# Output weights in two runs of 32 KB per partition, half the array's rows for each KV group, and three groups' projections in the bank of w2's sums

## The chip, the cores and the metric

The kernel runs on one core of a Trainium2 chip. The metric is the device time of one execution in microseconds (us), given as a median of several executions. The span of a profile is about 2 us shorter than the device time (before: 398.7 us of 400.74). The granted clock is the share of its full clock that PE was given, as the profile lists it.

Engines in the profile: PE is the matmul engine, PEld its weight loads, DVE, ACT and POOL the others, SPq the queue from which almost all transfers are issued. A transfer is spread over 16 transfer engines.

## The reference, cut to what matters

One token of a decode step: a layer norm, an attention with 32 query heads over 4 KV groups and 65,536 cached keys (k_cache and v_cache are 4 x 65536 x 128 in bf16, 67 MB each), an output projection, and beside it a small mixer with an MLP.

```python
def reference(A_x, A_k_cache, A_v_cache, A_wq, A_wo, B_x, B_w1, B_w2, B_w3, B_w4):
    # _A_ref: q = x @ wq; softmax(q k^T / sqrt(128)) v, 8 query heads per KV group;
    #         o.reshape(1, 1, 4096) @ wo                      wo: 4096 x 1024
    # _B_ref: h = gelu(ln(x) @ w1), shifted, @ w2; x1 = x + hs
    #         x1 + gelu(ln(x1) @ w3) @ w4                     w4: 3584 x 1024
    xn = _layernorm(x, axis=-1)
    return x + _A_ref(xn, ...) + _B_ref(xn, ...)
```

## The kernel before

Everything is read once through three slots of 64 KB per partition, in a fixed order: wq, w3, w1 and w2, then K and V tiles of 8.39 MB in turn, with wo between the last K and the last V, and w4 in four pieces at the end. A slot is loaded anew as soon as its user is done.

```python
W4_PIECES = (8, 14, 5, 1)
FIRST = 8
# ... cut ...
    stream = ["wq", "w3", "w12"]
    for u in range(NU):
        if u == NU - 1:
            stream += [("K", u), "wo", ("V", u)]
        else:
            stream += [("K", u), ("V", u)]
    stream.append("w4")
# ... cut: in Stream.load ...
            elif it == "wo":
                go(out=t[:].rearrange("p (g n) -> p g n", g=HKV),
                   in_=A_wo.rearrange("(g p j) n -> p g (j n)", g=HKV, p=P))
            elif it == "w4":
                w4_v = B_w4.rearrange("(m c) n -> m c n", c=FC)
                c0 = 0
                for n in W4_PIECES:
                    go(out=t[:, c0 * D:(c0 + n) * D], in_=w4_v[:, c0:c0 + n, :].rearrange("p c n -> p (c n)"))
                    c0 += n
```

The projections of groups 0 to 2 go, row by row, into a bank that the last scores also use; the last group's goes straight into the final sums (`quarter_acc`), as w4's products do.

```python
    def project(g):
        wt = st.tiles["wo"][:].rearrange("p (g j n) -> p g j n", g=HKV, j=8)
        for j in range(8):
            for h2 in range(2):
                if g == HKV - 1:
                    mm = quarter_acc(oT[g][:, j:j + 1], wt[:, g, j, 512 * h2:512 * (h2 + 1)], h2)
                    continue
                nc.tensor.matmul(tail["rows"][0:1, h2, :], lhsT=oT[g][:, j:j + 1],
                                 rhs=wt[:, g, j, 512 * h2:512 * (h2 + 1)], start=(g == 0 and j == 0),
                                 stop=(g == HKV - 2 and j == 7), tile_position=(0, 0))
        return mm.ins if g == HKV - 1 else None

    def quarter_acc(lhsT, row, j):
        for h in range(2):
            q = 2 * h + j
            mm = nc.tensor.matmul(quarters[h][32 * q:32 * q + 32, 0:256], lhsT=lhsT.to_broadcast([P, 32]),
                                  rhs=row[:, 256 * h:256 * (h + 1)], start=False, stop=False,
                                  tile_position=(0, 32 * q), skip_group_check=True)
        return mm
# ... cut ...
    compute_v(NU - 1, first_rows)                 # last V tile, then w4's first piece
    # ... then the last group's projection, then w4's pieces 2 to 4: compute_w4(8, 28), 80 matmuls
```

## Time and profile before

| | before |
|---|---|
| device time, first three runs | 400.97 us (400.63 to 401.44) |
| span of the profile | 398.7 us |
| last K tile landed | 340.57 us |
| wo landed | 323.68 + 36.3 = 360.0 us |
| last V tile's matmuls start | 379.43 us |
| w4's pieces 2 and 3 landed | 392.8 and 362.6 + 33.2 = 395.8 us |
| PE's last matmul ends | 396.84 us |

From the page of the kernel before: the first line, the engines' busy time, and the queue table (queue and kind, packets, MB, share of 16 engines' span).

```profile
span 398.7 us, 2684 instructions
...
PE 225.5 (57%) x1416; PEld 45.9 (12%) x922; DVE 210.7 (53%) x160; ACT 27.0 (7%) x35; POOL 5.8 (1%) x29
...
q1 hardware_dynamic: 3984, 169.87, 98.9%
q8 instruction: 9, 0.15, 0.1%
...
big<-in_A_wo_dram SPq DMA_DIRECT2D x1, 8192.0 KB, 36.3
...
big<-in_B_w_dram SPq DMA_DIRECT2D x1, 1280.0 KB, 33.2
```

The first queue is busy for 98.9% of the span: the kernel streams 170 MB and does all else beside it.

The chain of waits of before, its end (start, length, what):

```profile
362.16 30.64 DMA big<-in_B_w_dram
392.80 0.04 issue
392.84 4.05 PE pm_r L473 x80
396.89 0.02 issue
396.92 0.43 DVE out_t L520
```

PE waits for w4's second piece until 392.8 us and then goes through the 80 last matmuls in one sweep; pieces 3 and 4 land just in time. The matmuls on PE in that part (start, length, engine, line, operation, count, and in brackets the idle time before it and what ended it):

```profile
367.64 12.02 PE L455 MATMUL o_acc<-big,oT 128*1 128x512 bf16 x45 [2.40 <-ACT p_sb L380]
...
379.93 3.83 PE L412 MATMUL oacc<-big,p_sb 128*32 128x512 bf16 x58
...
387.96 1.06 PE L473 MATMUL pm_r<-big,oT 128*32 128x256 bf16 x32 [1.07 <-DVE oT L446]
392.84 4.00 PE L473 MATMUL pm_r<-big,hT 128*32 128x256 bf16 x80 [3.82 <-DMA big<-in_B_w_dram]
```

### The profile page before, as it was taken

To read this page: it belongs to the slowest core of one execution; us is meant where nothing else is said; L and a number is where in the kernel's file an instruction comes from. 1 tells how busy PE (TensorE), PEld (TensorE's weight loads), DVE (VectorE), ACT (ScalarE), POOL (GpSimd) and SP (SyncE) were. 2 spreads that over 40 slices of the span, in tenths; PEclk is the share of its full clock that TensorE was granted. 3 is DMA by queue.
4 is the path that set the end of the run, shared out by engine and by line. 5 is a ranking of instruction groups with operands and counts; after the bars stand their busy time and mean duration, and the time that the engine had idled before them with its cause. 6 is when DMAs were issued, how large, how long until landed. Compare 5 with 4: busy or idle time off the path is not lost.

```text
span 398.7 us, 2684 instructions
## 1 busy us (share of the span) xinstructions
PE 225.5 (57%) x1416; PEld 45.9 (12%) x922; DVE 210.7 (53%) x160; ACT 27.0 (7%) x35; POOL 5.8 (1%) x29
## 2 busy tenths in 40 slices
PE   0261960691668256923974196529552944394974
PEld 0210000010200120001001010200020101010133
DVE  0611010965196549653963895259439932894150
ACT  1001010003000200020002000200010011002000
POOL 2000000000000000000000000000000000000000
PEclk9995995597669666978796789568867997698896
DMA  9998999999999999999999999999999999999996
GB/s 421 421 443 382 439 441 473 447 421 421 416 435 421 441 447 455 421 421 427 436 421 427 454 454 427 416 427 427 434 436 454 434 434 388 419 452 426 418 432 252
DMA packets 4000, 170.03 MB, mean 426 GB/s; under 512 B 403, under 2 KB 405, under 8 KB 534
## 3 DMA queue, kind: packets, MB, share of 16 engines
q1 hardware_dynamic: 3984, 169.87, 98.9%
q8 instruction: 9, 0.15, 0.1%
q14 instruction: 1, 0.01, 0.0%
q10 hardware_dynamic: 6, 0.00, 0.0%
HBM read 169.87 MB, written 0.00 MB: 426 GB/s over the span
## 4 chain that ended last, share of the span: by engine, by line
DMA 55%; DVE 24%; PE 15%; ACT 2%; another core or an unknown queue 2%; issue 1%; SPq 0%; DVEq 0%; ACTq 0%
DMA big<-in_A_k_cache_dram 42%; DVE big L357 19%; PE sc L362 8%; DMA big<-in_B_w_dram 8%; DMA big<-in_A_wq_dram 5%; PE oacc L412 4%; DVE p_sb L383 2%; DVE mx L367 2%; ACT p_sb L380 2%; PE psq L287 2%; PE pm_r L473 1%; PE pm_mx L369 0%; DVE m L371 0%; PE pm_mx L376 0%
## 5 line engine op out<-in xcount | busy, mean ns | idle before, releaser
L362 PE MATMUL sc<-big,qdiag 128*128 128x512 bf16 x512 | 129.2, 413 | 65.5 <-DVE big L357 60.0
L357 DVE STREAM_TRANSPOSE big<-big 128x4096 f32<-128x4096 f32 x32 | 139.4, 4412 | 50.3 <-DMA big<-in_A_k_cache_dram 50.3
L412 PE MATMUL oacc<-big,p_sb 128*32 128x512 bf16 x512 | 44.9, 521 | 34.5 <-DVE p_sb L383 34.5
L367 DVE TENSOR_REDUCE mx<-sc 128x1 f32<-128x2048 f32 x8 | 18.3, 2292 | 29.8 <-PE sc L362 29.8
L362 PEld LDWEIGHTS <-qdiag 128*128 128x128 bf16 x128 | 13.2, 103 | 177.1 <-issue 145.6
L380 ACT ACTIVATE p_sb<-sc,nball 128x2048 bf16<-128x2048 f32 x8 | 15.7, 1967 | 220.0 <-DVE nball L378 219.9
L383 DVE STREAM_TRANSPOSE p_sb<-p_sb 128x2048 bf16<-128x2048 bf16 x8 | 18.5, 2311 | 18.0 <-ACT p_sb L380 18.0
L412 PEld LDWEIGHTS <-p_sb 128*32 128x32 bf16 x512 | 16.8, 126 | 59.5 <-DVE p_sb L383 35.1
L287 PE MATMUL psh<-big,ln_rep_b 128*32 128x512 bf16 (+1 forms) x64 | 12.4, 942 | 7.6 <-DMA big<-in_B_w_dram 7.6
L455 PE MATMUL o_acc<-big,oT 128*1 128x512 bf16 x48 | 12.7, 433 | 2.4 <-ACT p_sb L380 2.4
L369 PE MATMUL pm_mx<-ident_f,mx 128*1 128x128 f32 x8 | 2.3, 282 | 19.1 <-DVE mx L367 19.1
L421 DVE SCALAR_TENSOR_TENSOR og<-oacc,wb,og 128x512 f32<-128x512 f32 x4 | 3.0, 751 | 18.1 <-PE oacc L412 18.1
L326 DVE STREAM_TRANSPOSE h_row<-h_row 128x896 bf16<-128x896 bf16 x1 | 1.1, 1111 | 20.8 <-ACT h_row L325 20.8
L287 PE MATMUL psq<-big,ln_rep_a 128*32 128x512 bf16 x64 | 6.2, 575 | 3.8 <-DMA big<-in_A_wq_dram 3.8
L238 PE MATMUL pm_ln<-ln_rowsum_a,ones_f 128*128 128x1 f32 x2 | 0.6, 348 | 12.7 <-DVE ln_rowsum_a L236 12.7
L311 POOL COPY qdiag<-qx 32x32 bf16<-32x32 bf16 x16 | 3.2, 203 | 279.0 <-PE sc L362 249.8
L473 PE MATMUL pm_r<-big,hT 128*32 128x256 bf16 x112 | 5.1, 345 | 3.8 <-DMA big<-in_B_w_dram 3.8
L229 DVE STREAM_TRANSPOSE x_t<-x_row 32x256 bf16<-32x256 bf16 x4 | 2.5, 616 | 8.3 <-DMA x_row<-in_A_x_dram 8.2
L466 DVE TENSOR_TENSOR big<-o_acc,big 1x512 f32<-1x512 f32 x2 | 1.4, 680 | 9.8 <-PE o_acc L455 9.7
L434 PE MATMUL pm_e<-ol,sel8big 128*128 128x129 f32 x6 | 1.7, 372 | 7.9 <-DVE ol L432 7.9
L299 DVE CAST q_row<-psq 128x512 bf16<-128x512 f32 x1 | 0.7, 691 | 8.9 <-PE psq L287 8.9
L520 DVE CAST out_t<-pm_r 64x256 bf16<-64x256 f32 x1 | 0.4, 426 | 9.0 <-PE pm_r L473 9.0
(102 smaller groups left out, 72.6 us busy)
## 6 DMA issues: line engine op xcount, KB each, us to landing
big<-in_A_wo_dram SPq DMA_DIRECT2D x1, 8192.0 KB, 36.3
big<-in_B_w_dram SPq DMA_DIRECT2D x1, 7168.0 KB
big<-in_B_w_dram SPq DMA_DIRECT2D x3, 2048.0 KB, 43.9
big<-in_B_w_dram SPq DMA_DIRECT2D x1, 3584.0 KB, 30.6
big<-in_B_w_dram SPq DMA_DIRECT2D x1, 1280.0 KB, 33.2
big<-in_B_w_dram SPq DMA_DIRECT2D x1, 256.0 KB
big<-in_A_k_cache_dram SPq DMA_DIRECT2D x8, 41.8
big<-in_A_v_cache_dram SPq DMA_DIRECT2D x8, 36.9
```

The source lines that it names most:

```text
L229: nc.vector.transpose(out=x_t[32 * a:32 * a + 32].rearrange("p c j -> p (c j)"), in_=x_row[:, 256 * a:256 * (a + 1)].rearrange("p (i c) -> ...
L287: nc.tensor.matmul(acc[32 * q:32 * q + 32, i, 0:n], lhsT=rep[:, c, :], rhs=cols(c, i, q), start=(c == 0), stop=(c == DC - 1), tile_positio ...
L311: nc.gpsimd.tensor_copy(out=qdiag[at, LEAD:].rearrange("p (x c) -> p x c", x=4)[:, :, 32 * a:32 * a + 8], in_=qx[at, :, 8 * g:8 * g + 8])
L357: nc.vector.transpose(out=words, in_=words)
L362: nc.tensor.matmul(sc[:, e, :], lhsT=qdiag[:, c0:c0 + P], rhs=cols[:, s, e, :, b2, :, r], start=(s == 0 and b2 == 0 and r == 0), stop=(s = ...
L367: nc.vector.reduce_max(out=mx[:], in_=sc[:].rearrange("p e n -> p (e n)"), axis=AX.X)
L380: nc.scalar.activation(out=p_sb[:], in_=sc[:], func=ACTF.Exp, bias=nball[:, b:b + 1], scale=SCALE, accum_out=group["lall"][:, b:b + 1])
L383: nc.vector.transpose(out=flat, in_=flat)
L412: mm = nc.tensor.matmul(oacc[32 * q:32 * (q + 1), :], lhsT=pT[:, e, 32 * t:32 * (t + 1)], rhs=vt[:, :, e, t, :], start=(e == 0 and t < 4), ...
L421: nc.vector.scalar_tensor_tensor(out=og[:], in0=oacc[:], scalar=wb[:, 1:2], in1=og[:], op0=ALU.mult, op1=ALU.add)
L455: nc.tensor.matmul(tail["rows"][0:1, h2, :], lhsT=oT[g][:, j:j + 1], rhs=wt[:, g, j, 512 * h2:512 * (h2 + 1)], start=(g == 0 and j == 0), ...
L473: mm = nc.tensor.matmul(quarters[h][32 * q:32 * q + 32, 0:256], lhsT=lhsT.to_broadcast([P, 32]), rhs=row[:, 256 * h:256 * (h + 1)], start= ...
```

## The change

The intent: wo arrives in fewer and longer runs, two per partition of 32 KB; each KV group then owns 64 of the 128 partitions. The projections of groups 0 to 2 go as 32-column matmuls into the bank that already holds w2's sums, so they need not wait for the bank of the last scores, and two one-row additions on DVE go away.

```diff
             elif it == "wo":
-                go(out=t[:].rearrange("p (g n) -> p g n", g=HKV),
-                   in_=A_wo.rearrange("(g p j) n -> p g (j n)", g=HKV, p=P))
+                go(out=t[:].rearrange("p (g n) -> p g n", g=HKV // 2),
+                   in_=A_wo.rearrange("(g p j) n -> p g (j n)", g=HKV // 2, p=P))
# ... cut: masks for 64 rows; the gather of a group's rows writes 64 partitions ...
-    def project(g):
-        wt = st.tiles["wo"][:].rearrange("p (g j n) -> p g j n", g=HKV, j=8)
-        for j in range(8):
+    def project(g, rows, acc):
+        wt = st.tiles["wo"][:].rearrange("p (g j n) -> p g j n", g=HKV // 2, j=16)
+        for j in range(16):
             for h2 in range(2):
-                # ... cut: the two cases of before ...
+                mm = acc(h2, oT[g][rows, j:j + 1], wt[rows, g, j, 512 * h2:512 * (h2 + 1)])
+        return mm.ins
# ... cut ...
-        for j in range(2):
-            row = sums[32 * j:32 * j + 1, :]
-            nc.vector.tensor_tensor(out=row, in0=tail["rows"][0:1, j, :], in1=row, op=ALU.add)
# ... cut ...
-    for g in range(HKV - 1):
-        project(g)
+    project(0, slice(0, P), row_acc)
+    project(1, slice(0, 64), row_acc)
# ... cut ...
-        projected = project(HKV - 1)
+        projected = project(HKV // 2 - 1, slice(64, P), lambda h2, lhsT, w: quarter_acc(lhsT, w, h2))
```

More of the change, by code (lines that the diff above doesn't have):

```diff
@@ L266 @@
     nc.vector.tensor_reduce(out=sel8[:], in_=sel32[:].rearrange("p (j h) -> p h j", h=8), axis=AX.X, op=ALU.add)
-    mask16 = const.tile([P, 16], F32, name="mask16")
-    nc.vector.tensor_tensor(out=mask16[:], in0=sel32[:, 0:16], in1=sel32[:, 16:32], op=ALU.add)
     mask4 = const.tile([P, 4], F32, name="mask4")
     nc.vector.tensor_reduce(out=mask4[:], in_=sel32[:].rearrange("p (s h) -> p s h", h=8), axis=AX.X, op=ALU.add)
-    sel8big = const.tile([P, P], F32, name="sel8big")
-    nc.vector.tensor_copy(out=sel8big[:].rearrange("p (h d) -> p h d", d=16),
-                          in_=sel8[:].unsqueeze(2).to_broadcast([P, 8, 16]))
+    sel8big = const.tile([P, 64], F32, name="sel8big")
+    nc.vector.tensor_copy(out=sel8big[:].rearrange("p (h d) -> p h d", d=8),
+                          in_=sel8[:].unsqueeze(2).to_broadcast([P, 8, 8]))
     ln_s1 = const.tile([P, 1], F32, name="ln_s1")
@@ L428, in group_rows @@
     def group_rows(g, og, ol, fill):
-        pe = tail["rows"][:, 2, :] if fill else ps_M.tile([P, 512], F32, name="pm_e", tag="pm")
+        pe = (ps_S.tile([P, SUBS, 512], F32, name="pm_last", tag="sc")[:, 0, :] if fill
+              else ps_M.tile([P, 512], F32, name="pm_e", tag="pm"))
         own = og[:].rearrange("p (s d) -> p s d", d=DH)
@@ L432, in group_rows, with gather @@
         nc.vector.tensor_reduce(out=ol[:, 0:DH], in_=og[:].rearrange("p (s d) -> p d s", d=DH), axis=AX.X, op=ALU.add)
+        half = slice(64 * (g % 2), 64 * (g % 2) + 64)
+        def gather():
+            return nc.tensor.matmul(pe[half, 0:DH + 1], lhsT=sel8big[:], rhs=ol[:], start=True, stop=True,
+                                    tile_position=(0, 64 * (g % 2))).ins
         if fill is None:
-            nc.tensor.matmul(pe[:, 0:DH + 1], lhsT=sel8big[:], rhs=ol[:], start=True, stop=True)
+            gather()
@@ L435, in group_rows @@
         else:
             with tc.issue_after(fill()):
-                tail["gathered"] = nc.tensor.matmul(pe[:, 0:DH + 1], lhsT=sel8big[:], rhs=ol[:], start=True, stop=True).ins
-        msk = small.tile([P, 16, 8], F32, name="msk", tag="msk")
-        nc.vector.tensor_tensor(out=msk[:], in0=pe[:, 0:P].rearrange("p (dd j) -> p dd j", j=8),
-                                in1=mask16[:].unsqueeze(2).to_broadcast([P, 16, 8]), op=ALU.mult)
-        o5 = small.tile([P, 8], F32, name="o5")
-        nc.vector.tensor_reduce(out=o5[:], in_=msk[:].rearrange("p dd j -> p j dd"), axis=AX.X, op=ALU.add)
@@ L443, in group_rows @@
-        rl = small.tile([P, 1], F32, name="rl")
-        nc.vector.reciprocal(out=rl[:], in_=pe[:, P:P + 1])
-        oT[g] = const.tile([P, 8], BF16, name=f"oT{g}")
-        nc.vector.tensor_scalar(out=oT[g][:], in0=o5[:], scalar1=rl[:, 0:1], scalar2=None, op0=ALU.mult)
-    def project(g):
-        wt = st.tiles["wo"][:].rearrange("p (g j n) -> p g j n", g=HKV, j=8)
-        for j in range(8):
-            for h2 in range(2):
-                if g == HKV - 1:
-                    mm = quarter_acc(oT[g][:, j:j + 1], wt[:, g, j, 512 * h2:512 * (h2 + 1)], h2)
-                    continue
-                nc.tensor.matmul(tail["rows"][0:1, h2, :], lhsT=oT[g][:, j:j + 1],
-                                 rhs=wt[:, g, j, 512 * h2:512 * (h2 + 1)], start=(g == 0 and j == 0),
-                                 stop=(g == HKV - 2 and j == 7), tile_position=(0, 0))
-        return mm.ins if g == HKV - 1 else None
+                tail["gathered"] = gather()
@@ new lines, in group_rows @@
+        msk = small.tile([P, 8, 16], F32, name="msk", tag="msk")
+        nc.vector.tensor_tensor(out=msk[half], in0=pe[half, 0:P].rearrange("p (dd j) -> p dd j", j=16),
+                                in1=sel8[half].unsqueeze(2).to_broadcast([64, 8, 16]), op=ALU.mult)
+        o5 = small.tile([P, 16], F32, name="o5")
+        nc.vector.tensor_reduce(out=o5[half], in_=msk[half].rearrange("p dd j -> p j dd"), axis=AX.X, op=ALU.add)
+        rl = small.tile([P, 1], F32, name="rl")
+        nc.vector.reciprocal(out=rl[half], in_=pe[half, P:P + 1])
@@ new lines, in group_rows @@
+        if g % 2 == 0:
+            oT[g // 2] = const.tile([P, 16], BF16, name=f"oT{g // 2}")
+        nc.vector.tensor_scalar(out=oT[g // 2][half], in0=o5[half], scalar1=rl[half, 0:1], scalar2=None, op0=ALU.mult)
+    def project(g, rows, acc):
+        wt = st.tiles["wo"][:].rearrange("p (g j n) -> p g j n", g=HKV // 2, j=16)
+        for j in range(16):
+            for h2 in range(2):
+                mm = acc(h2, oT[g][rows, j:j + 1], wt[rows, g, j, 512 * h2:512 * (h2 + 1)])
+        return mm.ins
@@ L472, in quarter_acc @@
             q = 2 * h + j
-            mm = nc.tensor.matmul(quarters[h][32 * q:32 * q + 32, 0:256], lhsT=lhsT.to_broadcast([P, 32]),
+            mm = nc.tensor.matmul(quarters[h][32 * q:32 * q + 32, 0:256], lhsT=lhsT.to_broadcast([lhsT.shape[0], 32]),
                                   rhs=row[:, 256 * h:256 * (h + 1)], start=False, stop=False,
-                                  tile_position=(0, 32 * q), skip_group_check=True)
+                                  tile_position=(P - lhsT.shape[0], 32 * q), skip_group_check=True)
         return mm
@@ L491 @@
     compute_k(NU - 1)
-    tail["rows"] = ps_S.tile([P, SUBS, 512], F32, name="o_acc", tag="sc")
-    for g in range(HKV - 1):
-        project(g)
+    project(0, slice(0, P), row_acc)
+    project(1, slice(0, 64), row_acc)
     sums = copy_projection()
```

## The prediction

> **What bounds the kernel.** The transfer queue, from start to end: its packets took 98.9% of 16 engines' span (queue table). By the chain of waits, tiles of K land at 108.05, 185.65, 263.06 and 340.57 us: four 8.39 MB tiles per 77.4 to 77.6 us, so 19.4 us a tile, 433 GB/s. [...]
>
> The same stream gates the end. The output weights wo are issued at 323.7 us and take 36.3 us (table of DMA issues): landed at 360.0. The last V tile's matmuls start at 379.4. w4's second piece releases PE at 392.84, its third lands at 362.6 + 33.2 = 395.8, the last near 396.4 (the queue's own waits). The last four matmuls start at about 396.6 (timeline); two casts and the store end at 398.7.
>
> **What the change does.**
> - DMA: same bytes, same place in the queue; wo has 256 runs of 32 KB in place of 512 of 16 KB. In 16 KB runs it took 360.0 - 340.57 = 19.43 us; K and V in 64 KB runs take 19.35 to 19.4. Larger runs can win about 0.05 us; I count 0 to 0.1.
> - PE: 48 one-column matmuls (12.7 us busy, 367.6 to 379.9, kept back 2.4 us by the exponential, whose bank they need) become 64 of 32 columns in w2's bank. These don't wait for the exponential; I expect them from about 365.2 us, as pairs in two column tiles. w2's took 2.45 us for 8 pairs at full clock, 0.31 us a pair; at the half clock of 365 to 372 us I estimate 0.43 (one 512-column matmul's cadence there). So 32 pairs: 10 to 13 us, ending at 376 to 378, just before V lands.
> - DVE: two one-row additions (1.4 us, 380.1 to 381.5) and one constant go; the group's masks and reductions keep their length per partition.
> - The last group's projection grows from 32 matmuls (1.06 us) to 64 half-height ones: about 2.1 us, 3 at a low clock.
>
> **On the critical path: almost nothing.** After V's landing, the work before w4's second piece ends at about 389.0 us and PE idles 3.8 us (PE's waits). Cleaner V matmuls and DVE gain perhaps 0.3 us there, the doubled projection loses 1 to 2; both vanish in the 3.8 us. w4 is issued at 361.8 when K's slot comes free, 17 us before the queue would run dry; the change doesn't move that. So only wo's transfer counts: 400.97 - 0.1, about 400.8 us.
>
> **Predicted: 400.8 us, range 399.9 to 401.8** (runs before spread 0.8 us). Faster by over 2%: 0.01; within 2%: 0.98; slower: 0.01.
>
> **What the profile would show.** wo still lands 19.4 us after K's last tile; V's matmuls start near 379.4 with no projection matmuls among them; w4's second piece still releases PE near 392.8, after a wait of 2 to 3.5 us. Wrong, if the projections overrun 379.4 and the last group's end passes 392.8; or if wo's landing interval moves by over 0.3 us.
>
> **What would make it wrong.** Another rate of 32 KB runs (w1, w2 and the first K tile together show 416 GB/s from 38.9 to 69.1 us, a loss of about 1.1 us that I can't attribute; if 16 KB runs cost that, wo might save more than its landing shows). [...]

The sum is 400.97 us of before less 0.1 us for wo's longer runs, rounded to 400.8. The times given for the last group's doubled projection ("about 2.1 us, 3 at a low clock") are estimates: twice the 1.06 us of the 32 matmuls before, and for the 3 no source is named; measured were 1.95 us after and 3.27 us with one_column. They are not in the sum.

## The result, and the profile after

Six runs of each: 402.62 us after (401.90 to 402.73), 401.07 us before (400.63 to 401.44). The ratio is 1.0036, with a 95% interval of 1.0023 to 1.0049. A ratio here is the mean time of one kernel's runs over the mean of the other's in the same rounds, so it is not quite the ratio of the medians quoted. The kernel got slower by about 1.5 us: well within 2%, but outside the range of the prediction.

From the page after, the same lines:

```profile
span 400.6 us, 2803 instructions
...
PE 226.8 (57%) x1464; PEld 48.5 (12%) x994; DVE 209.3 (52%) x157; ACT 27.1 (7%) x35; POOL 5.8 (1%) x29
...
q1 hardware_dynamic: 3728, 169.87, 98.4%
q8 instruction: 9, 0.15, 0.1%
...
big<-in_A_wo_dram SPq DMA_DIRECT2D x1, 8192.0 KB, 36.9
...
big<-in_B_w_dram SPq DMA_DIRECT2D x1, 1280.0 KB, 34.6
```

PE has 48 matmuls and 72 weight loads more: 120 instructions. The packets of the first queue are 256 fewer, as intended, with the same bytes. w4's third piece, 1280 KB, now lands 34.6 us after its issue in place of 33.2.

The end of the chain of waits after, and PE's matmuls there:

```profile
362.68 34.56 DMA big<-in_B_w_dram
397.24 0.04 issue
397.29 1.52 PE pm_r L471 x24
398.81 0.02 issue
398.83 0.43 DVE out_t L517
```

```profile
365.36 9.98 PE L224 MATMUL psB<-big,oT 128*32 128x512 bf16 x64
...
379.40 6.23 PE L410 MATMUL oacc<-big,p_sb 128*32 128x512 bf16 x64 [4.06 <-DMA big<-in_A_v_cache_dram]
...
389.76 1.95 PE L471 MATMUL pm_r<-big,oT 64*32 64x256 bf16 x64 [1.05 <-DVE oT L452]
392.72 3.18 PE L471 MATMUL pm_r<-big,hT 128*32 128x256 bf16 x56 [1.01 <-DMA big<-in_B_w_dram]
397.29 1.47 PE L471 MATMUL pm_r<-big,hT 128*32 128x256 bf16 x24 [1.38 <-DMA big<-in_B_w_dram]
```

What the change touches went as planned, but for one thing without consequence: the last V tile's 64 matmuls took 6.23 us. PE had been idle for 4.06 us before them, and from 379.4 to 383.7 us it ran at a granted clock of 0.50; in the kernel before, where the projections ran right up to them, the clock there was 1.00. The projections are over by 375.3 us, the last V tile starts at 379.40 as before, the last group is done before w4's second piece, and that piece lands at 392.7 us as before. Only then do the kernels part: the third piece comes 1.4 us later, although neither it nor anything queued before it has changed in bytes or order.

The transfers by themselves, over the same two microseconds of the span after and before (the GB/s row is in 40 bins of 0.05 us, each packet counted in the bin in which it starts; 2 KB in one bin reads as 41):

```profile
core 0 of [0], span 400.6 us
DMA  0004000000010101101101010000000000000000
GB/s 0 0 0 205 0 0 0 0 0 0 0 41 0 41 0 41 41 0 41 41 0 41 0 41 0 0 0 0 0 0 0 0 0 0 0 0 0 0 0 0
DMA packets 11, 0.03 MB, mean 13 GB/s; under 512 B 2, under 2 KB 2, under 8 KB 10
```

```profile
core 0 of [0], span 398.7 us
DMA  0000000000000000000000000000000000000001
GB/s 0 0 0 0 0 0 0 0 0 0 0 0 0 0 0 0 0 0 0 0 0 0 0 0 0 0 0 0 0 0 0 0 0 0 0 0 0 0 0 41
DMA packets 2, 0.00 MB, mean 1 GB/s; under 512 B 0, under 2 KB 2, under 8 KB 2
```

This is the window 396.2 to 398.2 us. Before, every transfer engine is done by then; the two packets at the end are the store. After, one packet of 10 KB starts early in the window (the 205) and then 2 KB packets come one after the other, never two at a time: one engine is late by more than a microsecond, and the landing waited for it: this engine's last packet of the third piece ended at 396.80 us, those of the 15 others by 395.99, and PE resumed at 397.29.

Which engine, and why? The trace's packet records give start, length, queue and size of each packet, but no engine. Chains can be put together from the records by taking a packet that begins some nanoseconds from another's end as the next on the same engine (1 to 14 ns in the two chains below); that is an inference. This is the late engine of the kernel after (us from the span's start, length in ns, queue, bytes):

```
 392.152   392  q1  10240      w4's third piece
 392.540   388  q1  10240
 392.925   388  q1  10240
 393.309  1073  q8  16384      a fetch of instructions
 394.368   875  q1  10240      the packet right after it
 395.240   389  q1  10240
 395.626   ...                 10,240 B packets to 396.79, then w4's fourth piece, done at 397.45
```

and this is the engine of the ninth fetch in the kernel before:

```
 395.439    84  q1  2048       w4's fourth piece
 395.522    87  q1  2048
 395.605     9  q1  4          its completion
 395.611  1029  q8  16384      a fetch of instructions, after all the data
```

In both traces there are nine such fetches of 16,384 B, spread over the whole span. In every one that falls into the stream, the fetch takes 0.95 to 1.1 us of its engine, and the data packet right after it takes about 0.5 us longer than others of its size (875 ns for 388 here; 64 KB packets 2,885 to 2,967 for 2,420). So a fetch costs its engine about 1.55 us (1.07 for the ninth in the chain after, and 0.49 more for the packet behind it; an estimate from these records). When do the 16 engines finish?

| engines finish at (us of the span) | before | after |
|---|---|---|
| engines with no fetch | seven: 393.9 to 394.4 | seven: 394.2 to 394.6 |
| one engine, later by one packet of another kind (see the last section) | 395.2 | 395.2 |
| engines with one fetch in their data | eight: 395.6 to 396.1 | seven: 395.7 to 396.0 |
| engine with two | none | one: 397.45 |

The groups follow from the finishing times and the size of a step, not from a record of the engine. That leads to the theory.

**Theory.** The nine fetches of 16,384 B bring PE's instructions, and they are carried by the same transfer engines as the data. Eight engines take them in turn (by the groups above: eight engines late by one step before; seven by one step and one by two after), so the ninth falls on one that has had the first. With 120 more instructions on PE ahead of the end, the ninth block is fetched before w4 is all in (at 393.31 us), rather than just after (395.61). (That the fetches are PE's is tested below by adding instructions to PE.) That engine has then lost time twice, ends 1.5 us after the others, and w4's last pieces wait for it.

**Rivals.** The runs of 32 KB might bring the engines out of step. Or something in the new projections (half-height matmuls, the shared bank, more PE work in the tail) might cost the time.

### The profile page after: what moved, and what is told of

The parts are those of the page before. It is cut to its first block, busy times and chain, and to the rows that moved or that the text cites. A ratio compares the mean times of both kernels' runs of the same rounds, so it can differ in the third digit from the quotient of the medians.

```text
span 400.6 us, 2803 instructions
## 1 busy us (share of the span) xinstructions
PE 226.8 (57%) x1464; PEld 48.5 (12%) x994; DVE 209.3 (52%) x157; ACT 27.1 (7%) x35; POOL 5.8 (1%) x29
## 4 chain that ended last, share of the span: by engine, by line
DMA 56%; DVE 21%; PE 18%; ACT 2%; another core or an unknown queue 2%; issue 1%; SPq 0%; DVEq 0%; ACTq 0%
DMA big<-in_A_k_cache_dram 42%; DVE big L355 15%; PE sc L360 11%; DMA big<-in_B_w_dram 9%; DMA big<-in_A_wq_dram 5%; PE oacc L410 4%; DVE p_sb L381 2%; DVE mx L365 2%; ACT p_sb L378 2%; PE psq L285 1%; PE pm_r L471 0%; PE pm_mx L367 0%; DVE m L369 0%; PE pm_mx L374 0%
## 5 line engine op out<-in xcount | busy, mean ns | idle before, releaser
L410 PE MATMUL oacc<-big,p_sb 128*32 128x512 bf16 x512 | 46.5, 543 | 38.6 <-DVE p_sb L381 34.5
L224 PE MATMUL psB<-big,oT 128*32 128x512 bf16 (+1 forms) x64 | 10.0, 483 | 0.0
L435 PE MATMUL pm_e<-ol,sel8big 128*64 128x129 f32 x6 | 1.7, 382 | 7.9 <-DVE ol L431 7.9
L471 PEld LDWEIGHTS <-hT 128*32 128x32 bf16 x112 | 4.2, 129 | 3.8 <-issue 3.3
## 6 DMA issues: line engine op xcount, KB each, us to landing
big<-in_A_wo_dram SPq DMA_DIRECT2D x1, 8192.0 KB, 36.9
big<-in_B_w_dram SPq DMA_DIRECT2D x1, 1280.0 KB, 34.6
big<-in_A_v_cache_dram SPq DMA_DIRECT2D x8, 36.9
```

Of the source, the lines that this page charges most:

```text
L224: return nc.tensor.matmul(psB[32 * j:32 * j + 32, :], lhsT=lhsT.to_broadcast([lhsT.shape[0], 32]), rhs=rhs, start=start, stop=False, tile_ ...
L410: mm = nc.tensor.matmul(oacc[32 * q:32 * (q + 1), :], lhsT=pT[:, e, 32 * t:32 * (t + 1)], rhs=vt[:, :, e, t, :], start=(e == 0 and t < 4), ...
```

## The experiments

Each kernel was run in five rounds beside the kernel before, in three sets, each with its own runs of before: wo_runs_alone, pad_120, one_column and pad_24 on one chip (before: 400.95 us); pad_376, pads_8_x_283 and low8_before on another (401.15 us); pad_48, after_again and after_16k_runs later, on a chip listed under the same number (400.84 us). Three of the kernels compute a wrong projection. Their outputs are wrong, which doesn't matter for the times. The comparison with the reference passed them all the same, so it hardly sees the projection; that matters for reading "correct" in this case, not for the times.

### The runs of wo alone

```diff
 # on the kernel before
-                go(out=t[:].rearrange("p (g n) -> p g n", g=HKV),
-                   in_=A_wo.rearrange("(g p j) n -> p g (j n)", g=HKV, p=P))
+                go(out=t[:].rearrange("p (g n) -> p g n", g=HKV // 2),
+                   in_=A_wo.rearrange("(g p j) n -> p g (j n)", g=HKV // 2, p=P))
```

> The kernel before, with wo's transfer alone in two runs of 32 KB (the result is wrong on purpose: the projection still reads the old layout). Fetch theory (PE has 120 more instructions, so the ninth 16 KB fetch of instructions falls into w4's stream and holds up one transfer engine that had the first fetch as well): nothing changes, ratio to before 0.999 to 1.001, about 401.0 us, the ninth fetch again after that engine's last w4 packet. Rival (32 KB runs bring the engines out of step, one ends late): about 402.5 us, ratio 1.003 to 1.005, one engine ending over 1 us after the others.

Measured: 401.04 us against 400.95, ratio 0.9997 (0.9983 to 1.0011). The ninth fetch began at 395.88 us, when its engine was done. The longer runs neither cost nor gain anything that can be measured.

### 120 instructions more (and one weight load), and nothing else

```diff
 # on the kernel before
+    pad = ps_M.tile([P, 512], F32, name="pm_pad", tag="pm")
+    for _ in range(120):
+        nc.tensor.matmul(pad[0:32, 0:1], lhsT=xn2_rep[:, 0, :], rhs=xn2_rep[:, 1, 0:1], start=True, stop=True,
+                         tile_position=(0, 0))
     for u in range(NU - 1):
```

> The kernel before, with 120 one-column matmuls and one weight load added while PE waits for the first K tile (result right; wo, projections and tail untouched). Fetch theory: the whole loss comes with them: 402.3 to 402.8 us, ratio 1.003 to 1.005; the ninth fetch starts some 393 us into the span, and the engine that carries it ends 1.3 to 1.6 us after all others. Rivals (runs of wo, or the projection's new matmuls): 401.0 us, ratio within 0.001 of 1.

Measured: 402.06 us against 400.95, ratio 1.0027 (1.0015 to 1.0040). The scheduler placed the matmuls at 29.9 to 32.9 us, 360 us ahead of the end, where they hold up nothing. The ninth fetch began at 388.90 us, and one engine ended at 397.39, 1.5 us after all others. Its last microseconds, in the same window as above, look like those of the kernel after:

```profile
core 0 of [0], span 400.0 us
DMA  0040000000101101011011000000000000000000
GB/s 0 0 205 0 0 0 0 0 0 0 41 0 41 41 0 41 0 41 41 0 41 41 0 0 0 0 0 0 0 0 0 0 0 0 0 0 0 0 0 0
DMA packets 11, 0.03 MB, mean 13 GB/s; under 512 B 2, under 2 KB 2, under 8 KB 10
```

The loss comes with the instructions, without wo's new layout and without the new projections. The sizes were missed a little: the time is 0.24 us under the range expected and 0.5 us under the kernel after, which is taken up below, and the ninth fetch came some 4 us earlier than expected.

### The kernel after with before's number of instructions

```diff
 # on the kernel after: the same column for all j, so that the kernel's own pass drops repeated weight loads
-                mm = acc(h2, oT[g][rows, j:j + 1], wt[rows, g, j, 512 * h2:512 * (h2 + 1)])
+                mm = acc(h2, oT[g][rows, 0:1], wt[rows, g, j, 512 * h2:512 * (h2 + 1)])
```

> The kernel after, with every projection matmul taking the same column of weights, so that 120 weight loads are dropped at build and PE is back at before's instruction count, with all matmuls, tiles and transfers of the kernel after (wrong result on purpose). Fetch theory: 400.8 to 401.3 us, ratio to before 0.999 to 1.001; the ninth fetch again after that engine's last w4 packet, no late engine. Rivals (half-height projections, the shared bank, wo's runs): 402.3 to 402.8 us as the kernel after.

Measured: 400.84 us against 400.95, ratio 0.9998 (0.9986 to 1.0011). All matmuls (1464), banks and transfers of the change are there. The weight loads are 874 in place of 994, so that PE has 2,338 instructions, as in the kernel before (1416 + 922). The loss is gone. The ninth fetch began at 395.89 us, after its engine's data; all engines ended by 395.91. PE's last 80 matmuls run through again without a second wait:

```profile
392.65 4.14 PE L471 MATMUL pm_r<-big,hT 128*32 128x256 bf16 x80 [1.04 <-DMA big<-in_B_w_dram]
```

Adding the instructions alone makes the loss, taking them away from the change removes it.

### A small dose

The pad with 24 matmuls in place of 120.

> As the padded kernel, with 24 matmuls in place of 120: a small dose. In the trace of before the ninth fetch started within 0.01 us of the end of its engine's last w4 packet, and PE goes through the last w4 matmuls at 39 instructions per us. Fetch theory: 24 instructions bring the fetch forward by about 0.6 us, into the last pieces: over half of the loss already, 401.7 to 402.6 us. If cost were proportional to the added instructions or PE time: 24/120 of 1.55 us, 401.3 us. Rivals: 401.0 us.

Measured: 401.35 us against 400.95, ratio 1.0006 (0.9994 to 1.0019). A miss: I expected over half of the loss. The ninth fetch began at 395.75 us, within 0.01 us of the end of its engine's data, just as in the kernel before, though by the theory PE asks for it earlier. In before, in this kernel and in the two without a loss, the fetch begins within 0.01 us of its engine's running out of data, so I take it that it had been waiting for that. How long a fetch waits behind data that is already queued on its engine, no record shows; if it did wait, it was for longer than I had reckoned, and there was more room left than I thought. The median alone would also fit a cost in proportion to the instructions (I had named 401.3 us for that). The trace speaks against it: all transfers ended by 395.97 us, as in the kernel before (396.08), and the profiled run is 0.4 us longer than the one before because its last 80 matmuls took 4.55 us in place of 4.00, with a granted clock of 0.50 to their end.

### 48

The pad with 48 matmuls.

> The kernel before with 48 added one-column matmuls. With 24 the ninth fetch still began only when its engine had nothing left to carry (395.75 us); with 120 it began at 388.9. By the counts, 48 make PE reach the fetching instruction at about 393.2 us. Fetch theory: the fetch begins between 393.5 and 395 us, before that engine's w4 packets are done, and the loss is there in full: 402.2 to 402.8 us, ratio 1.003 to 1.005, for 40% of the added instructions. If the cost grew with the number of instructions: 48/120 of 1.1 us, 401.4 us.

Measured: 402.62 us against 400.84, ratio 1.0037 (1.0023 to 1.0051): the whole loss, as large as that of the change (1.0036 in the same rounds). The ninth fetch began at 392.13 us, earlier than expected (393.2 was an estimate from instruction counts), and one engine ended at 397.42. Between 24 and 48 instructions the cost goes from nothing that can be told from noise to all of it. It is a step, not a slope.

### More fetches: 376 matmuls, and 8 times 283

First the pad with 376:

> The kernel before with 376 one-column matmuls in place of the 120: one more fetch than with 120, ten in all. In the traces so far the first eight fetches go to eight engines, and the ninth to the engine of the first. Fetch theory with that order: the tenth goes to the engine of the second, so two engines end late together, at about 397.4 us of the span, and the time is no longer than with 120: 401.9 to 402.6 us. If it were the number of instructions or the PE time that cost: 376/120 of 1.1 us, 404.4 us.

Measured: 402.68 us against 401.15, ratio 1.0033 (1.0020 to 1.0046). The median is 0.08 us over the range. The page counts ten fetches, and two engines ended late together, at 397.2 and 397.3 us. Three times the instructions of 120, two late engines in place of one, and no step more.

Then the same matmuls in eight places:

```diff
 # on the kernel before
+    def pad():
+        scrap = ps_M.tile([P, 512], F32, name="pm_pad", tag="pm")
+        for _ in range(283):
+            nc.tensor.matmul(scrap[0:32, 0:1], lhsT=xn2_rep[:, 0, :], rhs=xn2_rep[:, 1, 0:1], start=True, stop=True,
+                             tile_position=(0, 0))
+
+    pad()
     for u in range(NU - 1):
         compute_k(u)
         compute_v(u)
+        pad()
```

> The kernel before with 283 one-column matmuls in each of eight places: at the start and after each V tile but the last, 2264 in all, 25 ns each. Fetch theory: 17 or 18 fetches; every one of the eight engines has two, one or two have three, and those end about 1.5 us later again, near 399 us of the span: 403.4 to 404.2 us. The transfer queue must stay full throughout (K tiles landing every 19.4 us); if PE's added 57 us kept it waiting, K would land later and this run would not count.

Measured: 403.77 us against 401.15, ratio 1.0067 (1.0054 to 1.0080). From its page:

```profile
q8 instruction: 18, 0.29, 0.3%
```

Seventeen fetches fell into the stream, the eighteenth came after its engine's data. The engines ended in groups again: seven at 393.9 to 394.4 us, one at 395.2, seven at 397.15 to 397.55, one at 398.94. That is what two fetches on each of eight engines give, with a third on one of them. The last K tile landed at 342.05 us, 1.5 us later than before: the late engines set that landing too, so this is the theory's own effect, and PE's added work did not keep the queue waiting. I had written that the run would not count if PE's work made K land late, so this needs showing: the K tiles that landed before the ninth fetch (221 us) came as in the kernel before (DVE can start on them at 108.19 and 185.60 us, before: 108.05 and 185.65), and both after it came 1.5 us late (264.55 and 342.05 for 263.06 and 340.57), by one round of fetches and no more. Fetches taken in turn by eight engines, about 1.5 us each, the slowest engine setting the end: one count explains when the transfers end with 0 to 2,264 added instructions.

### A part of a transfer given to eight engines only

```diff
 # on the kernel before, in w4's load
-                    go(out=t[:, c0 * D:(c0 + n) * D], in_=w4_v[:, c0:c0 + n, :].rearrange("p c n -> p (c n)"))
+                    parts = [(0, 96)] + [(r, r + 8) for r in range(96, P, 8)] if n == 5 else [(0, P)]
+                    for lo, hi in parts:
+                        go(out=t[lo:hi, c0 * D:(c0 + n) * D], in_=w4_v[lo:hi, c0:c0 + n, :].rearrange("p c n -> p (c n)"))
```

> The kernel before (no added matmuls), with w4's third piece, 10 KB per partition, split: partitions 0 to 95 by one transfer (16 engines, 6 partitions each), 96 to 127 by four transfers of 8 partitions each, which use 8 engines only. Those 8 carry 10 partitions of the piece, the other 8 carry 6: 20 KB more and 20 KB less than before, 0.75 us each at 27 GB/s. In all traces 8 engines end at about 394.1 us, the 8 that carried fetches at about 395.9. If the 8 chosen are those without fetches: both groups end near 395, and the time falls by 0.6 to 0.8 us, to 400.2 to 400.5. If they are those with fetches: they end near 396.7, and the time rises by as much, to 401.6 to 401.9. Unchanged time would speak against the theory that the end is set by the engine with most to carry.

Measured: 407.32 us against 401.15, ratio 1.0158 (1.0144 to 1.0172). Neither outcome that I had named. (The 27 GB/s in the expectation is the rate of one engine's 64 KB packets in the kernel before, 65,536 B in 2,420 ns.) The small parts did go to eight engines each: the queue shows 432 completions for 400 before, 32 more for four transfers. But the 10 KB packets of the piece took 818 ns at the median, in the kernel before 387: the split slowed the packets themselves. The run therefore says nothing about which eight engines carry the fetches, and giving the idle engines more bytes was not pursued.

### The kernel after again, and with the runs of before

The kernel after, unchanged, on the chip of the 48 and of the next one:

> The kernel after, unchanged, on the same chip as the two others: 402.4 to 402.8 us, one transfer engine ending near 397.4 us of the span.

Measured: 402.56 us against 400.84, ratio 1.0036 (1.0023 to 1.0049); one engine ended at 397.36 us.

Then the kernel after with wo's transfer of before:

```diff
 # on the kernel after
-                go(out=t[:].rearrange("p (g n) -> p g n", g=HKV // 2),
-                   in_=A_wo.rearrange("(g p j) n -> p g (j n)", g=HKV // 2, p=P))
+                go(out=t[:].rearrange("p (g n) -> p g n", g=HKV),
+                   in_=A_wo.rearrange("(g p j) n -> p g (j n)", g=HKV, p=P))
```

> The kernel after with wo's transfer in four runs of 16 KB as before (wrong result on purpose: the projections read the new layout). Fetch theory: as the kernel after, ratio to it within 0.001, 402.4 to 402.8 us. If the 32 KB runs had a part in the loss, some of it goes: under 402.2 us.

Measured: 402.73 us against 400.84, ratio 1.0042 (1.0030 to 1.0055). The loss stays without the long runs. With the first experiment this shuts out wo's layout from both sides.

### Half a microsecond more or less

The kernels after, pad_48 and pad_120 end their transfers within 0.06 us of each other (397.45, 397.42 and 397.39 us), but pad_120 is 0.5 us faster. The clock granted to PE, in the stretch in which it catches up with w4's last chunks, differs. After, then pad_120 (stretch, its length, busy time and count of each engine, granted clock, DMA share, GB/s):

```profile
397.25:398.80 1.55, 1.47 (x24) 0.85 (x23) 0.00 (x0) 0.01 (x1) 0.00 (x0) 0.50 0.01 3
```

```profile
397.20:398.20 1.00, 0.93 (x24) 0.63 (x23) 0.00 (x0) 0.01 (x1) 0.00 (x0) 1.00 0.01 4
```

In the first the last 24 matmuls ran at half clock (0.50, busy for 1.47 us), in the second at full (1.00, 0.93 us). What sets the clock was not shown. So the loss in the two profiled runs, 400.6 - 398.7 = 1.9 us, is 1.4 us of the late engine (397.45 - 396.08) and about 0.5 us of catching up at half clock. That second part was read from the profiles and not tested by a run of its own, and it varies: runs of the kernel after lie between 401.90 and 402.73 us. The other profiles bear it out. From the last transfer's end to the end of the span it takes 3.13 to 3.18 us where PE's last matmuls ran at 0.50 (after, after_again, after_16k_runs, pad_24, pad_48), and 2.60 to 2.71 us where they ran at 0.98 to 1.00 (before, wo_runs_alone, one_column, pad_120).

## Why the prediction was wrong

- **What bounds the kernel: right.** The stream sets the time throughout, and its end sets the end.
- **wo's transfer: right.** It landed at 322.98 + 36.9 = 359.9 us, 19.4 us after the last K tile, as before; alone it changed the time by a ratio of 0.9997.
- **The projections of groups 0 to 2: right.** Expected from 365.2 us to 376 or 378; they ran from 365.36 to 375.34, with none left among the last V tile's matmuls.
- **The tail before w4's second piece: right that it fits, wrong in size.** The wait left over was 1.0 us, not 2 to 3.5, because the V tile's matmuls, which the prediction had as slightly faster, took 6.23 us where the kernel before had some 4.3 (granted clock 0.50 for 1.00); w4's second piece still came at 392.7.
- **The step that failed:** "So only wo's transfer counts", resting on "same bytes, same place in the queue". The bytes of the data are the same, but the transfer engines also carry PE's instructions (nine fetches of 16,384 B in each of the two traces). The change adds 120 of them, and with that moves one 16 KB fetch from behind the data into it, on an engine that had lost time to an earlier one. I had costed the added matmuls and weight loads only as time on PE. "q8 instruction: 9" was on the profile of before. The count alone would not have warned: it is 9 after the change as well, and only the time of the ninth differs (393.31 us for 395.61).
- **The listed risk:** another rate of 32 KB runs was not the cause (a ratio of 0.9997 for wo's runs alone). The loss of 1.1 us that I could not attribute, between 38.9 and 69.1 us, lies where the first fetch falls (42.86 us in before, on an engine that the first K tile's landing then waits for); a fetch costs its engine about 1.55 us. No run was made to test this, but three traces agree with it: with pad_120, pad_376 and pads_8_x_283 the first fetch comes at 34.0 to 36.1 us, before w3 is in; PE's matmuls on w3 then resume at 40.1 to 40.2 us in place of 38.9, while DVE begins on the first K tile at 69.3 to 69.6 us, hardly later than before (69.2). The loss has moved ahead of 38.9 us with the fetch.

No kernel here beats the one before. The change without its added instructions is level with it, because all eight engines that carry fetches have one each in any case, and they end at 396 (395.91 us with one_column, 396.08 before).

## What to carry to other kernels

In this kernel, bound by its transfers (98.9% of the span), instructions were transfers too: blocks of 16 KB, each on one of 16 engines, nine for PE's 2,338 instructions and nine more for 2,264 added ones (about 250 instructions a block, an estimate from these counts). The landing of w4's third piece waited for the slowest engine. 120 matmuls added to PE at 29.9 us, where they held up nothing, made the kernel 1.1 us slower by way of a transfer that ended at 397.39, and the cost came in one step (ratio 1.0006 with 24, 1.0037 with 48). (Other engines' instructions were not tried.) So, where a kernel is bound by its transfers, look at the number of instruction packets, at where the last of them falls, and at whether the last GB/s of the stream come from all engines or from one.

## What the traces show of the fetches and the transfer engines

- The cost of a fetch is not hidden from the transfers: each fetch in the stream took 0.9 to 1.1 us of one engine, and the data packet behind it about 0.5 us more. The ninth fetch made the kernel 1.1 to 1.9 us slower (ratios 1.0027 to 1.0042) when it fell into the stream. There were 9, 10 and 18 fetches of 16,384 B for 0, 376 and 2,264 added matmuls.
- On which engines the fetches (queue q8 in this trace) go, no record says. By the finishing times here, eight of 16 take them in turn: ten fetches left two engines late, seventeen in the stream left the eight level with two and one of them with three.
- Once begun, a fetch stands between two whole data packets of the trace here (from 393.309 us, for 1,073 ns, between two of 10,240 B). But with data still queued it may wait: in five kernels a fetch began within 0.01 us of its engine's running dry, and 24 more instructions ahead of it did not bring it forward (395.75 us for 395.61).
- Delays of one engine were not made up in the stream here: the two groups of engines were about 1.7 us apart at 394 to 396 us (393.9 to 394.4, and 395.6 to 396.1), by fetches of which the first lay at 43 us. One 8 KB load on another queue (q14, which the trace also calls instruction), at 113 us, seems to show in the same way: the data packet behind it took 3,080 ns for 2,420, and one engine ended at 395.2 us, 0.8 us after the group without fetches. That the two are the same engine is inferred.
- With this very split of a load by partitions (one part of 96, four of 8) 10 KB packets took 818 ns in place of 387, and the kernel 1.6% longer. Why the packets were slow was not tested.
